# Attention low halves ahead of the feed-forward evacuations, late bounds and moved norms in a fused attention and feed-forward kernel

## The chip, the cores and the metric

One core of a Trainium2 chip runs the whole program. The metric is the time on the device in microseconds (us), as the median of several runs. TensorE (PE) multiplies and transposes, VectorE (DVE), ScalarE (ACT) and GpSimd (POOL) work beside it, and SyncE (SP) issues most DMAs. Each engine takes its instructions strictly in the order in which the program emitted them.

## The reference

The queries are averaged in pairs, so that each of 32 heads (4 batches of 8) has 576 queries against 1152 keys of dimension 64. After the softmax the heads of a batch are laid side by side (512 columns), normalized, and put through a feed-forward layer of width 2048 with a residual.

```python
q_pool = q.reshape(B, H, S // 2, 2, D).mean(axis=3)
scores = scale * np.matmul(q_pool, k.transpose(0, 1, 3, 2))
attn = np.exp(scores - np.max(scores, axis=-1, keepdims=True))
attn = attn / (np.sum(attn, axis=-1, keepdims=True) + 1e-09)
x = np.matmul(attn, v)                      # (4, 8, 576, 64) -> (4, 576, 512)
xn = (x - mu) / np.sqrt(var + 1e-06) * g_ln
out = x + np.maximum(xn @ w_ch1, 0.0) @ w_ch2
```

## The kernel before

**Work.** Every fp32 operand of a matmul is split into a scaled fp16 high half and an fp16 low half, and three products (high by high, high by low, low by high) stand for one. The heads go in 16 pairs p (`HP` = 4 pairs a batch), and a pair has `C` = 9 blocks of 128 queries, so there are 144 attention steps i = 9 p + j. `step(i)` writes out one step for all engines.

**A step.** VectorE takes the row maximum of the scores (`emit_max`, line 399) and makes the exponential's bias `nb` (line 404). ScalarE does the exponential (line 413) and the high half (`emit_hi`, line 427). The low half (`emit_lo`) falls on GpSimd for j = 2, 5, 8 (first a multiplication by 2^15 in place, line 254, then the subtraction, line 434), else on VectorE (line 436). SyncE then issues a transposing DMA, and four steps later TensorE multiplies with the values (`emit_pv`, line 482). In the first 36 steps (`on_pe`, pairs 0 to 3) TensorE transposes the probabilities instead (line 446), ScalarE copies them out (line 452), the product comes out turned and is turned back (`emit_turn`, line 498), and the result is scaled by 1/sum (line 530, then line 537 on ScalarE). VectorE converts the weights in these steps (`w_conv`, through `drip`, line 111).

**Order on TensorE** from step 36 on: scores of block i + 1 (lines 380 and 388), a reduction matmul for a pair's bounds if one is due (lines 206 and 215, `reds`), the product with the values, transposes for a coming pair's keys and queries (`prep_k`, `prep_q`, lines 294, 298, 323, 333), one piece of feed-forward work (`some_units`: `l1` line 618, `l2` line 650), then what `todo` holds: loads, bounds on ScalarE (line 190), and transposes of a normalized block (`ln_t`, line 581).

**Evacuations.** What TensorE leaves in PSUM in step i is collected in `evacs` and written out by `flush` in step i + 1, ahead of the exponential. There are two free banks, 6 and 7 (`bank()`), for transposes, units and norms together; a second-layer unit holds its bank over two steps. Scores use three banks for even and three for odd steps. The product with the values and the two reduction matmuls lie in columns 128 to 386 of the third of these, whose first 128 columns are the end of the scores (line 388).

**Bounds.** `all_max` turns a pair's three partial sums on TensorE (line 206), VectorE takes their maximum (line 209) and spreads it over a small diagonal `dg` (line 210), TensorE multiplies it with ones (line 215), and `scales` makes powers of two of it, which the transposes of keys and queries and the values need.

**Norms.** Once the eight pieces of a block of 128 rows are there, `norm` takes statistics on VectorE (line 563), GpSimd normalizes, and two steps later `ln_t` transposes. Blocks are called t = 0 to 3 for a batch; t = 1 and t = 3 release feed-forward units. After step 143 only feed-forward work is left.

Of the kernel before, what the change touches and what calls it, by code (L numbers as in the profile page):

```python
# [24 lines left out]
def tile_pooled_attention_moe(  # L25
# [18 lines left out]
    nc = tc.nc  # L44
# [150 lines left out]
    def all_max(src, n, then):  # L195

        mx = sm_p.tile([3, 1], FP32, tag="mx3", name="mx3")
        dg = sm_p.tile([3, 3], FP32, tag="dg", name="dg")

        def place():  # L200
            u = this[0] if on_pe(this[0]) else pv_slot[0]
            return psum[:, 3 * (u % 2) + 2, 258:386]

        def one():
            ps = place()
            nc.tensor.transpose(ps[0:n], src, ident)

            def evac():
                nc.vector.tensor_reduce(mx[0:n], ps[0:n], axis=AX.X, op=ALU.max)
                nc.vector.tensor_scalar(dg[0:n, 0:n], ident[0:n, 0:n], mx[0:n], None, op0=ALU.mult)  # L210
            return evac

        def two():
            ps = place()
            nc.tensor.matmul(out=ps[:, 0:n], lhsT=ones3[0:n], rhs=dg[0:n, 0:n], start=True, stop=True)
            return lambda: then(ps[:, 0:n])

        return one, two
# [12 lines left out]
    def scales(p, top, a=0, b=3, both=False):  # L231
# [12 lines left out]
        if a == 0:  # L244
            v.scalar_tensor_tensor(
                sc[:, 0:1], e[:, 0:1], 2.0 ** -32, e[:, 1:2], op0=ALU.mult, op1=ALU.mult
            )
            if on_pe(p * C):
                v.scalar_tensor_tensor(
                    sc[:, 1:2], e[:, 0:1], -(2.0 ** -32), e[:, 1:2], op0=ALU.mult, op1=ALU.mult  # L250
                )

# [87 lines left out]

    def preps_of(p):
        if p < JOINT:
            return PREPS
        if p % 2:
            return [x for x in PREPS if x[0] is prep_k]
        x = PREPS + ((prep_q, 3), (prep_q, 4))
        return x if p != HP else x[:3] + (x[4], x[3]) + x[5:]
# [47 lines left out]
    def emit_max(i):  # L395
# [5 lines left out]
        if on_pe(i):  # L401
            st["mx"] = mx
        else:
            nc.vector.tensor_scalar(nb, mx, sc[:, 0:1], -1.0, op0=ALU.mult, op1=ALU.mult)  # L404

# [18 lines left out]
    def emit_hi(i):  # L424
        st = steps[i]
        hl = st["hl"] = p_p.tile([128, 2, S], FP16, tag="hl", name="hl", bufs=3)
        nc.scalar.activation(out=hl[:, 0], in_=st["pe"], func=ACTF.Copy, scale=2.0 ** 15)  # L427

    def emit_lo(i):
        st = steps[i]  # L430
        hl = st["hl"]
        if low_on_pool(i):
            scaled(st["pe"], st["pe"], 2.0 ** 15)
            nc.gpsimd.tensor_tensor(hl[:, 1], st["pe"], hl[:, 0], op=ALU.subtract)  # L434
# [54 lines left out]

    turned, scaled_out = deque(), deque()  # L490

    def emit_turn(n, ot, i):
# [6 lines left out]
        one, two = evac_pv(n, ps)  # L499
        found.append(one)  # L500
        scaled_out.extend((two, lambda: evacuated(n)))

# [3 lines left out]
    def evac_pv(i, ps):  # L506
# [28 lines left out]
        def two():  # L535
            for u in range(m):
                nc.scalar.activation(  # L537
                    out=x[:, 64 * u:64 * u + 64], in_=ps[o:o + n, 65 * u:65 * u + 64],
                    func=ACTF.Copy, scale=r[:, u:u + 1],
                )  # L540

# [50 lines left out]
    units, preps = deque(), deque()  # L592
    evacs = []

    def flush():
        mine, evacs[:] = list(evacs), []
        waiting.clear()
        for fn in mine:
            fn()
            drip()  # L600
# [227 lines left out]
    for p in range(1, NP):  # L828
# [5 lines left out]
        else:  # L834
            lk = i0 - 2 if p % 2 or not ahead else i0 - 3
        at(lk, load, p, "k", nc.sync)
        at(i0 - ahead, load, p, "v", nc.sync)
        at(i0 + 1 if old else i0, bound, p, "k")
        if p == 1:
# [26 lines left out]
        for n, (fn, u) in enumerate(preps_of(p)):  # L866
            if p == JOINT - 1 and n > 3:
                n -= 1
            pre(i0 + 4 + n + late, lambda fn=fn, p=p, u=u: preps.append((fn, p, u)))
# [46 lines left out]
    def norm(i):  # L916

        if not norms or norms[0][1] % 2 == 0 and norms[0][0] != "h" and not room["xn"]:
            return
        b, t = norms.popleft()  # L920
        st = {}
# [13 lines left out]
        def transpose():  # L935
            evacs.extend(ln_t(st, dst))

# [34 lines left out]
    def some_units(i):  # L972
        for _ in range(1 if i < NSTEP + 5 else 2):
            if units and w_done[units[0][0]] >= units[0][1]:
                evacs.extend(units.popleft()[2]())

    def a_piece(i):
        pieces.extend(ready.pop(i, ()))
        for u in range(2 if len(pieces) > 2 and not on_pe(i) else 1):
            if pieces:  # L980
# [10 lines left out]
                evacs.extend(evac_pv(n, ps))  # L991
                evacs.append(lambda n=n: evacuated(n))

    def step(i):
# [14 lines left out]
        if on_pe(i):  # L1009
# [4 lines left out]
            emit_exp(i)  # L1014
        while scaled_out:
            scaled_out.popleft()()
        if i + 1 < NSTEP:
# [11 lines left out]
        else:  # L1029
            flush()  # L1030
            if live:
                emit_exp(i)
                emit_hi(i)
        if 0 <= i - 1 < NSTEP and not on_pe(i - 1):
            emit_lo(i - 1)
            steps.pop(i - 1)
            drip()
        norm(i)
        while soon or len(fill) > 3:
            drip()  # L1040
        if on_pe(i):
            emit_t(i)
            if reds:
                found.append(reds.popleft()())
        elif reds:
            evacs.append(reds.popleft()())
# [3 lines left out]
        if not on_pe(i):  # L1050
            if not first:
                a_piece(i)
            for _ in range(max(len(preps), 1)):
                a_prep()
            some_units(i)
        for fn, a in todo.pop(i, ()):
            fn(*a)
# [6 lines left out]
    with tc.manual_schedule():  # L1064
# [50 lines left out]
        i = 0  # L1115
        while i < NSTEP + 20 or units or evacs or norms:
            step(i)
# [30 lines left out]
```

## Time and profile before

| | |
|---|---|
| time, median of 3 runs | 913.89 us (908.51 to 914.88) |
| the profiled execution's own time | 909.41 us |
| its span, first to last instruction | 907.4 us |
| mean granted TensorE clock | 0.983 |
| TensorE busy (matmul) | 826.9 us, 91% |
| VectorE, ScalarE, GpSimd busy | 624.7, 569.6, 361.6 us (69%, 63%, 40%) |
| the chain that ended last, by engine | PE 40%, DVE 31%, ACT 16%, DMA 5%, issue 5%, POOL 2% |

An engine's busy time is the sum over its instructions in one profiled execution, and its share is taken of the span. The granted clock is 1.00 at 2.4 GHz and 0.50 at 1.2 GHz. An idle time in brackets behind an instruction is the engine's wait just before it, with the instruction that ended it.

### The profile page before, as it was taken

The page shows a single profiled execution, that of the slowest core. Times are in us where ns is not written, and L with a number is a line of the kernel's source. Part 1 is how long each engine was busy: PE and PEld are TensorE (multiplying, and loading weights), DVE is VectorE, ACT ScalarE, POOL GpSimd, SP SyncE. Part 2 cuts the span into 40 slices and gives each one's busy share as a digit, 9 for nine tenths or more (in the row PEclk, how much of TensorE's full clock was granted, in tenths as well). Part 3 has the DMA queues.
Part 4 walks back from the last instruction along what each step waited for, and adds up shares of the span by engine and source line. Part 5 has one row for each costly group of instructions (what it writes and reads, how often), then busy time and mean ns, then how long its engine had stood idle before and what let it go on. Part 6 is the DMA issues. An engine that isn't in the chain of part 4 may idle for free.

```text
span 907.4 us, 21663 instructions
## 1 busy us (share of the span) xinstructions
PE 826.9 (91%) x9180; PEld 584.8 (64%) x9180; DVE 624.7 (69%) x1087; ACT 569.6 (63%) x850; POOL 361.6 (40%) x324
## 2 busy tenths in 40 slices
PE   8998897998789988797999999898989999999997
PEld 6787776776546564654666666466657576766764
DVE  3688989797877786576777777877777777641211
ACT  4998696887657756566766667576767766511110
POOL 3020927257859726262633334444624342400000
PEclk9999899899999999898999999999999999999999
DMA  7374425304676877776796969587888876600001
GB/s 191 136 213 127 148 84 163 119 26 94 121 163 129 185 140 143 164 155 136 147 176 114 194 134 186 111 179 132 162 157 147 162 129 131 131 20 12 13 12 24
DMA packets 276017, 115.97 MB, mean 128 GB/s; under 512 B 259280, under 2 KB 259280, under 8 KB 275920
## 3 DMA queue, kind: packets, MB, share of 16 engines
q1 hardware_dynamic: 275568, 113.70, 59.2%
q8 instruction: 72, 1.18, 0.6%
q10 hardware_dynamic: 352, 0.88, 0.4%
q14 instruction: 25, 0.20, 0.1%
HBM read 46.14 MB, written 4.72 MB: 56 GB/s over the span
## 4 chain that ended last, share of the span: by engine, by line
PE 40%; DVE 31%; ACT 16%; DMA 5%; issue 5%; POOL 2%; SPq 0%; ACTq 0%; POOLq 0%; DVEq 0%
PE psum L650 12%; PE psum L618 10%; DVE mx L399 9%; DVE hl L436 6%; ACT pe L413 4%; PE psum L470 4%; PE psum L482 4%; DMA pt<-hl 3%; PE psum L380 3%; DVE ht L632 3%; PE psum L446 2%; DVE stage L111 2%; ACT ht L631 2%; ACT qt L283 2%; DVE dg L210 1%
## 5 line engine op out<-in xcount | busy, mean ns | idle before, releaser
L413 ACT ACTIVATE pe<-psum,nb,sc 128x1152 f32<-128x1152 f32 x144 | 188.9, 1312 | 36.8 <-DVE nb L404 26.1
L399 DVE TENSOR_REDUCE mx<-psum 128x1 f32<-128x1152 f32 x144 | 194.3, 1349 | 25.3 <-PE psum L482 12.9
L650 PE MATMUL psum<-wsl,ht 128*128 128x512 f16 x864 | 197.8, 381 | 1.9 <-DVE xb L663 0.8
L618 PEld LDWEIGHTS <-wsl 128*128 128x128 f16 x1920 | 172.6, 99 | 24.1 <-issue 4.4
L618 PE MATMUL psum<-xn,wsl 128*128 128x256 f16 x1536 | 180.3, 276 | 1.5 <-DVE ht L632 0.8
L650 PEld LDWEIGHTS <-ht 128*128 128x128 f16 x864 | 83.0, 98 | 92.3 <-issue 4.7
L427 ACT ACTIVATE hl<-pe 128x1152 f16<-128x1152 f32 x108 | 125.7, 1163 | 9.8 <-DMA pt<-hl 6.5
L380 PE MATMUL psum<-kt,qt 64*128 64x512 f16 (+1 forms) x960 | 121.8, 380 | 3.2 <-ACT pe L413 2.3
L482 PE MATMUL psum<-vt,pt 128*128 128x65 f16 (+1 forms) x3240 | 118.4, 194 | 0.0
L482 PEld LDWEIGHTS <-pt 128*128 128x128 f16 (+1 forms) x3240 | 110.3, 101 | 2.3 <-issue 0.2
L436 DVE SCALAR_TENSOR_TENSOR hl<-pe,hl 128x1152 f16<-128x1152 f32 x72 | 108.8, 1512 | 3.5 <-ACT hl L427 3.5
L537 ACT ACTIVATE xb<-psum,r 128x64 f32<-128x64 f32 x128 | 39.4, 308 | 113.7 <-DVE r L533 110.3
L254 POOL TENSOR_SCALAR pe<-pe 128x1152 f32<-128x1152 f32 x36 | 42.1, 1169 | 163.0 <-ACT hl L427 151.0
L632 DVE SCALAR_TENSOR_TENSOR ht<-psum,ht 128x512 f16<-128x512 f32 x72 | 49.7, 690 | 75.1 <-ACT ht L631 74.7
L631 ACT ACTIVATE ht<-psum 128x512 f16<-128x512 f32 x72 | 42.8, 594 | 88.9 <-PE psum L618 88.7
L434 POOL TENSOR_TENSOR hl<-pe,hl 128x1152 f16<-128x1152 f32 x36 | 86.4, 2399 | 3.0
L470 PE MATMUL psum<-pt,vt 128*65 128x128 f32 (+1 forms) x720 | 80.5, 269 | 1.4 <-DVE qt L280 1.4
L470 PEld LDWEIGHTS psum<-pt,vt 128*65 128x65 f32 x720 | 74.6, 142 | 1.8 <-DVE qt L280 1.8
L380 PEld LDWEIGHTS <-qt 64*128 64x128 f16 (+1 forms) x960 | 34.3, 96 | 55.7 <-issue 36.2
L388 PEld LDWEIGHTS <-qt 128*128 128x128 f16 (+1 forms) x320 | 17.9, 99 | 72.5 <-issue 72.0
L280 DVE SCALAR_TENSOR_TENSOR qt<-psum,s,qt 128x512 f16<-128x512 f32 (+2 forms) x43 | 28.5, 663 | 42.7 <-ACT qt L283 42.7
L388 PE MATMUL psum<-kt,qt 128*128 128x128 f16 (+1 forms) x320 | 41.4, 226 | 12.1 <-ACT xb L537 10.5
(119 smaller groups left out, 1021.9 us busy)
## 6 DMA issues: line engine op xcount, KB each, us to landing
stage<-in_moe_w_ch_dram SPq DMA_DIRECT2D x32, 512.0 KB, 5.1
kr<-in_k_dram SPq DMA_DIRECT2D x16, 576.0 KB, 4.7
qraw<-in_q_dram SPq DMA_DIRECT2D x31, 288.0 KB, 5.0
vr<-in_v_dram SPq DMA_DIRECT2D x15, 576.0 KB, 4.9
out_dram<-xb SPq DMA_DIRECT2D x32, 128.0 KB, 2.4
pt<-hl SPq DMA_TRANSPOSE x108, 4.6
kr<-in_k_dram SPq DMA_DIRECT2D x16, 64.0 KB, 4.3
vr<-in_v_dram ACTq DMA_DIRECT2D x1, 576.0 KB, 6.8
```

The lines of the kernel that those rows point to most:

```text
L380: nc.tensor.matmul(out=sp[o:o + w, c0:c0 + 512], lhsT=qt[r:r + 64, qa, c:c + w], rhs=kt[r:r + 64, ka, h], start=(a == 0), stop=(a == 2),)
L399: nc.vector.tensor_reduce(mx, st["s"], axis=AX.X, op=ALU.max)
L413: nc.scalar.activation(out=st["pe"], in_=st["s"], func=ACTF.Exp, scale=pair[i // C]["sc"][:, 0:1], bias=st["nb"],)
L427: nc.scalar.activation(out=hl[:, 0], in_=st["pe"], func=ACTF.Copy, scale=2.0 ** 15)
L434: nc.gpsimd.tensor_tensor(hl[:, 1], st["pe"], hl[:, 0], op=ALU.subtract)
L436: nc.vector.scalar_tensor_tensor(hl[:, 1], st["pe"], 2.0 ** 15, hl[:, 0], op0=ALU.mult, op1=ALU.subtract)
L470: nc.tensor.matmul(out=ps[0:65, q0:q0 + w], lhsT=vt[:, h, c], rhs=pt[:, 128 * u + q0:128 * u + q0 + w], start=(u == 0), stop=(u == C - 1),)
L482: nc.tensor.matmul(out=dst[:, 0:n], lhsT=lhsT, rhs=rhs, start=(u == 0 and lhsT is hi and n == 65), stop=(u == C - 1 and lhsT is lo), skip_ ...
L618: nc.tensor.matmul(out=ps[:, o:o + n], lhsT=wsl[:, 8 * w + cc, wa, f * 128:f * 128 + 128], rhs=xn[:, xa * KD + cc, 0:n], start=(m == 0), s ...
L631: lambda: nc.scalar.activation(out=hi, in_=pv, func=ACTF.Relu),
L632: lambda: nc.vector.scalar_tensor_tensor(lo, pv, 0.0, hi, op0=ALU.max, op1=ALU.subtract),
L650: nc.tensor.matmul(out=ps, lhsT=hv[0][:, ha, f, t * 128:t * 128 + 128], rhs=wsl[:, 8 * w + 4 + f // 2, wa, (f % 2) * DM:(f % 2) * DM + DM] ...
```

## The change

`flush` now has two lists: `evacs` (product with the values, transposes of keys and queries) goes first, then the attention's low half of step i - 1, then `lates` (units, norms, and bounds from step 54 on). From step 54 on (`JOINT` = 6 pairs) the bounds' reduction matmuls are emitted behind the unit. `dg` is made from PSUM in one operation with two tensor inputs. In the first 36 steps 1/sum is applied on VectorE, right after it is formed. On GpSimd's blocks the factor 2^15 goes into the exponential's bias, so the multiplication on line 254 falls away. Pair 5's transposes come one a step, its second key transposes last; pair 6's loads of keys and values move two steps and one step back, the bound of its keys one; the last two query transposes of a pair of pairs come one step later; norms with t > 1 wait until i % 9 is at least 5.

```diff
             def evac():
                 nc.vector.tensor_reduce(mx[0:n], ps[0:n], axis=AX.X, op=ALU.max)
-                nc.vector.tensor_scalar(dg[0:n, 0:n], ident[0:n, 0:n], mx[0:n], None, op0=ALU.mult)
+                nc.vector.scalar_tensor_tensor(
+                    dg[0:n, 0:n], ps[0:n, 0:n], mx[0:n], ident[0:n, 0:n], op0=ALU.max, op1=ALU.mult
+                )
...
-            if on_pe(p * C):
-                v.scalar_tensor_tensor(
-                    sc[:, 1:2], e[:, 0:1], -(2.0 ** -32), e[:, 1:2], op0=ALU.mult, op1=ALU.mult
-                )
+            v.scalar_tensor_tensor(
+                sc[:, 1:2], e[:, 0:1], -(2.0 ** -32), e[:, 1:2], op0=ALU.mult, op1=ALU.mult
+            )
...
     def preps_of(p):
+        if p == JOINT - 1:
+            return PREPS[:3] + PREPS[4:] + PREPS[3:4]
...
-            nc.vector.tensor_scalar(nb, mx, sc[:, 0:1], -1.0, op0=ALU.mult, op1=ALU.mult)
+            up = 15 * math.log(2) if low_on_pool(i) else 0.0
+            nc.vector.tensor_scalar(nb, mx, sc[:, 1:2], up, op0=ALU.mult, op1=ALU.add)
...
-        nc.scalar.activation(out=hl[:, 0], in_=st["pe"], func=ACTF.Copy, scale=2.0 ** 15)
+        up = 1.0 if low_on_pool(i) else 2.0 ** 15
+        nc.scalar.activation(out=hl[:, 0], in_=st["pe"], func=ACTF.Copy, scale=up)
...
         if low_on_pool(i):
-            scaled(st["pe"], st["pe"], 2.0 ** 15)
             nc.gpsimd.tensor_tensor(hl[:, 1], st["pe"], hl[:, 0], op=ALU.subtract)
...
-        found.append(one)
-        scaled_out.extend((two, lambda: evacuated(n)))
+        found.extend((one, two, lambda: evacuated(n)))
...
-                nc.scalar.activation(
-                    out=x[:, 64 * u:64 * u + 64], in_=ps[o:o + n, 65 * u:65 * u + 64],
-                    func=ACTF.Copy, scale=r[:, u:u + 1],
-                )
+                src, dst = ps[o:o + n, 65 * u:65 * u + 64], x[:, 64 * u:64 * u + 64]
+                if on_pe(i):
+                    nc.vector.tensor_scalar(dst, src, r[:, u:u + 1], None, op0=ALU.mult)
+                else:
+                    nc.scalar.activation(out=dst, in_=src, func=ACTF.Copy, scale=r[:, u:u + 1])
...
-    evacs = []
-
-    def flush():
-        mine, evacs[:] = list(evacs), []
+    evacs, lates = [], []
+
+    def flush(between=None):
+        first, last = list(evacs), list(lates)
+        evacs.clear()
+        lates.clear()
         waiting.clear()
-        for fn in mine:
+        for fn in first:
+            fn()
+            drip()
+        if between:
+            between()
+        for fn in last:
             fn()
             drip()
...
-            lk = i0 - 2 if p % 2 or not ahead else i0 - 3
+            lk = i0 - 3 * ahead + p % 2
         at(lk, load, p, "k", nc.sync)
-        at(i0 - ahead, load, p, "v", nc.sync)
-        at(i0 + 1 if old else i0, bound, p, "k")
+        at(i0 if old else i0 + 1 - 2 * ahead, load, p, "v", nc.sync)
+        at(i0 if ahead else i0 + 1, bound, p, "k")
...
         for n, (fn, u) in enumerate(preps_of(p)):
-            if p == JOINT - 1 and n > 3:
-                n -= 1
+            if u > 2:
+                n += 1
             pre(i0 + 4 + n + late, lambda fn=fn, p=p, u=u: preps.append((fn, p, u)))
...
-        b, t = norms.popleft()
+        b, t = norms[0]
+        if i < NSTEP and (b == "h" or t > 1) and i % C < 5:
+            return
+        norms.popleft()
...
         def transpose():
-            evacs.extend(ln_t(st, dst))
+            lates.extend(ln_t(st, dst))
...
             if units and w_done[units[0][0]] >= units[0][1]:
-                evacs.extend(units.popleft()[2]())
+                lates.extend(units.popleft()[2]())
...
+    def low(n):
+        if 0 <= n < NSTEP and not on_pe(n):
+            emit_lo(n)
+            steps.pop(n)
+            drip()
...
-            flush()
+            flush(lambda: low(i - 1))
             if live:
                 emit_exp(i)
                 emit_hi(i)
-        if 0 <= i - 1 < NSTEP and not on_pe(i - 1):
-            emit_lo(i - 1)
-            steps.pop(i - 1)
-            drip()
...
-        elif reds:
+        elif reds and i < JOINT * C:
             evacs.append(reds.popleft()())
...
             some_units(i)
+            if reds and i >= JOINT * C:
+                lates.append(reds.popleft()())
```

## Rows read from the trace of the kernel before

**Rows 1.** Windows: stretch, length, busy time and instructions by engine, granted clock, DMA.
```profile
63.00:120.00 57.00, 49.60 (x485) 41.66 (x483) 50.10 (x77) 46.35 (x88) 25.36 (x20) 0.94 0.40 125
...
340.00:390.00 50.00, 42.76 (x500) 27.66 (x498) 31.68 (x58) 31.02 (x41) 23.30 (x17) 0.93 0.73 147
...
690.00:740.00 50.00, 49.78 (x614) 34.27 (x610) 38.90 (x70) 36.78 (x51) 17.31 (x14) 1.00 0.84 154
```
**Rows 2.** Waits over the span: total us, times, longest us.
```profile
DVE ht L632 <- ACT ht L631: 74.7, 48, 3.4
...
PE psum L215 <- DVE dg L210: 11.5, 7, 2.6
...
PE psum L388 <- ACT xb L537: 10.5, 11, 1.9
...
PE psum L298 <- DVE kt L280: 9.4, 7, 2.8
...
PE psum L581 <- DVE qt L280: 3.9, 4, 1.9
...
PE psum L581 <- DVE xb L663: 2.7, 1, 2.7
```
**Rows 3.** Timeline 468 to 492, steps 83 to 87: start, length, instruction, [idle before].
```profile
468.74 2.78 PE L618 MATMUL psum<-xn,wsl 128*128 128x256 f16 x24
...
471.35 2.38 DVE L210 TENSOR_SCALAR dg<-ident,mx 3x3 f32<-3x3 f32 x1
471.36 2.36 POOL L434 TENSOR_TENSOR hl<-pe,hl 128x1152 f16<-128x1152 f32 x1
...
473.79 0.38 PE L215 MATMUL psum<-dg,ones 3*128 3x3 f32 x2 [1.27 <-DVE dg L210]
...
485.64 0.44 PE L298 MATMUL psum<-ident,kr 128*128 128x128 f32 x2 [1.26 <-DVE kt L280]
```
**Rows 4.** Four lines' instructions: shortest, median, longest ns, first and last start.
```profile
L399 DVE TENSOR_REDUCE mx<-psum x144: 1323/1348/1359, 16.0 to 778.2; 128x1 f32<-128x1152 f32 x144
...
L210 DVE TENSOR_SCALAR dg<-ident,mx x20: 201/217/2385, 11.0 to 713.5; 3x3 f32<-3x3 f32 x13, 1x1 f32<-1x1 f32 x4, 2x2 f32<-2x2 f32 x3
...
L632 DVE SCALAR_TENSOR_TENSOR ht<-psum,ht x72: 679/692/694, 222.0 to 893.0; 128x512 f16<-128x512 f32 x72
...
L436 DVE SCALAR_TENSOR_TENSOR hl<-pe,hl x72: 1345/1349/3066, 210.0 to 781.7; 128x1152 f16<-128x1152 f32 x72
```
**Rows 5.** Timeline 331 to 432, TensorE, steps 65, 73 and 75.
```profile
366.80 0.38 PE L206 MATMUL psum<-ident,acc 128*3 128x128 f32 x1 [3.90 <-ACT kt L190]
...
368.46 4.52 PE L618 MATMUL psum<-xn,wsl 128*128 128x256 f16 x24
...
417.43 0.63 PE L581 MATMUL psum<-ident,xs 128*128 128x128 f32 x4 [2.69 <-DVE xb L663]
...
423.50 0.58 PE L215 MATMUL psum<-dg,ones 3*128 3x3 f32 x2 [2.23 <-DVE dg L210]
...
425.47 5.01 PE L618 MATMUL psum<-xn,wsl 128*128 128x256 f16 x24
```
**Rows 6.** Timeline 226 to 262, TensorE, step 43.
```profile
252.58 0.90 PE L323 MATMUL psum<-ident,qraw 64*128 64x64 f32 x6 [4.18 <-DVE kt L280]
```
**Rows 7.** Timeline 66 to 86, step 11.
```profile
67.37 1.31 ACT L413 ACTIVATE pe<-psum,nb,sc 128x1152 f32<-128x1152 f32 x1
...
68.94 0.27 PE L388 MATMUL psum<-kt,qt 128*128 128x128 f16 x2 [0.79 <-ACT xb L537]
...
69.05 1.15 PE L446 MATMUL psum<-ident,pe 128*128 128x128 f32 x9
```
**Rows 8.** Costliest groups of the page: busy us, mean ns, idle before.
```profile
L537 ACT ACTIVATE xb<-psum,r 128x64 f32<-128x64 f32 x128 | 39.4, 308 | 113.7 <-DVE r L533 110.3
L254 POOL TENSOR_SCALAR pe<-pe 128x1152 f32<-128x1152 f32 x36 | 42.1, 1169 | 163.0 <-ACT hl L427 151.0
```
**Rows 9.** DMA issues of the page: count, size, us to landing.
```profile
vr<-in_v_dram SPq DMA_DIRECT2D x15, 576.0 KB, 4.9
```

More of the change, by code (lines that the diff above doesn't have):

```diff
@@ L1 @@
+import math
 from collections import deque
@@ L488, in emit_pv @@
         return ps
-    turned, scaled_out = deque(), deque()
+    turned = deque()
     def emit_turn(n, ot, i):
@@ L1014, in step @@
             emit_exp(i)
-        while scaled_out:
-            scaled_out.popleft()()
         if i + 1 < NSTEP:
@@ L1115, in tile_pooled_attention_moe @@
         i = 0
-        while i < NSTEP + 20 or units or evacs or norms:
+        while i < NSTEP + 20 or units or evacs or lates or norms:
             step(i)
```

## The prediction

> **What bounds the kernel now.** I read the windows first [rows 1]. Between 690 and 740 us, late in the attention, TensorE is busy for 49.78 of 50.00 us, with VectorE at 38.90 and ScalarE at 36.78: a step can be written so that TensorE never waits, and neither of the others stands in the way. Between 340 and 390 us the same kind of steps leaves TensorE idle for 7.24 us, at a granted clock of 0.93. So TensorE's work sets the time, and the change, which takes nothing from that work, can win only its gaps and the stretches at 1.2 GHz. The gaps are in the list of waits [rows 2]. Each has a name: TensorE waits at line 215 for `dg` (11.5 us, 7 times), at line 388 for ScalarE's scaling of a block in the same bank (10.5 us, 11 times), at line 298 for the low half of the first keys (9.4 us, 7 times), at line 581 for a bank that the last transposes or unit still hold (6.6 us in two rows). Last I read the timelines of single steps [rows 3, 5 to 7] to see what would be late next.
>
> In the stage with both attention and feed-forward work, VectorE is the one that is late, though it is busy only 78% even in the best window. It stands still for ScalarE's ReLU before each unit's low half (74.7 us, 48 times [rows 2]), with the attention's low half queued behind that wait, and behind this the next step's maximum. Now the edits, with their share against the profiled execution's 909.41 us.
>
> **Bounds: `dg` and the matmuls behind the unit.** `dg` has 3 columns and a median of 217 ns, but a longest of 2385 [rows 4]. In step 84 it took 2.38 us exactly beside GpSimd's 2.36 us of line 434, and TensorE, whose line 215 stood ahead of the values and the unit, waited 1.27 us [rows 3]; in step 75 it waited 2.23 [rows 5]. The new form reads PSUM and one tensor in SBUF. The nearest row of that form is line 632, and all its 72 instructions lie between 679 and 694 ns, many of them beside GpSimd [rows 4]; so I take 0.2 us for the new one (0.2 to 2.4 as bounds). The matmuls still run, but behind 2.78 us of unit, by when `dg` is ready. The 7 waits of line 215 go: 11.5. In step 65 line 206 waited 3.90 us for a bound on ScalarE [rows 5]; behind the unit it would not hold up TensorE, but ScalarE's exponential stays late, so I count half, 2. **Together -13** (0 to -15.4).
>
> **TensorE's clock.** The unit behind these two waits ran at 1.2 GHz: 24 matmuls in 4.52 and 5.01 us against 2.78 in step 83 [rows 3, 5], so 1.7 and 2.2 us lost on the unit alone, and about a third more on the step's other 2 us of matmuls. In both cases TensorE had stood still for over 2 us just before. If the waits go, these two stretches should too: **-4** (0 to -5.5).
>
> **Pair 5's transposes one a step.** Today its second keys and a third of its queries come in the same step, while a second-layer unit holds the other bank, and the queries waited 4.18 us for the keys' low half [rows 6]. That goes. The price is pair 6's loads: keys now come at the end of step 45 and their bound at the end of 46, values at the end of 46 and their bound at the end of 47, one step from issue to use instead of two. SyncE also waits there for the last key transposes, with a transposing DMA queued behind it that nobody needs for four steps. A value load lands 4.9 us after its issue [rows 9], about as long as a step; ScalarE, with the exponential queued behind the bound, may wait 0 to 4.9 us twice. I take 1.5. **-2.7** (-4.2 to +5.6).
>
> **Norms and late query transposes.** In step 73 the block's transposes waited 2.69 us because the query transposes and the unit had both banks [rows 5]; in all line 581 waits 6.6 us in these rows [rows 2]. Moving the query transposes out of j = 1, and the norms of t = 2 and 3 so that `ln_t` falls on j = 7 and 8, where the coming odd pair has no transposes left, clears all but the wait of t = 0 (two steps behind j = 6, beside a coming even pair's query transposes). The norm's statistics and GpSimd's part move along. The units of t = 3 come two steps later, but the 16 of t = 1 last longer than that. **-5** (0 to -6.6).
>
> **Low half first.** The low half needs ScalarE's `hi` of the step before, always there ahead of this step's ReLU, which is queued behind it on ScalarE; so it fills the wait of line 632. I worked steps 84 to 87 through by hand with the durations of the rows. VectorE reaches the first keys' low half 1.3 us sooner relative to TensorE, since the `dg` stretch is gone, the bounds' scales no longer stand ahead of 1/sum, and the wait is filled; line 298's 1.26 us [rows 3] falls away. In return the unit's low half ends up to 1.35 us (line 436 [rows 4]) later, and the next unit, in the same bank, waits 0.2. As line 298's waits are partly the echo of line 215's, of their 9.4 us I count **-5** (0 to -9.4), and **+2** for units that wait for their bank (0 to +10).
>
> **First 36 steps: 1/sum on VectorE.** The 10.5 us of line 388 look like a gain, but only part is one. In step 11 the scores' end waited 0.79 us, yet the transposes behind it need the exponential, which ended at 68.68, 0.37 us before they began [rows 7]: the exponential is late next. So 0.3 to 0.5 us come back each time, and ScalarE, which paces that chain, loses 308 ns a step [rows 8]. VectorE gains 40 small operations, between `dg`'s 0.2 and the 512 columns' 0.69 us [rows 4]; I take 0.25 for 64 columns, 10 us in all, and it is busy 50.10 of 57 us there [rows 1]. Where weights are converted beside GpSimd's splits, this is paid in full. **-2.5** (-10 to +10).
>
> **2^15 in the bias.** 36 operations of 1.17 us leave GpSimd [rows 8], whose blocks reach the transposing DMA that much sooner, four steps ahead of use: **-1** (0 to -3). The bias costs what it cost. The 12 more operations on `sc` take about 0.2 us each, in VectorE's idle time.
>
> Sum: -13 - 4 - 2.7 - 5 - 5 + 2 - 2.5 - 1 = -31.2, so 878.2 for a profiled execution. The median of the runs is 4.5 above that execution's own time: **883**.
>
> **Rivals.** *The bank is held.* In the rows line 388 waits for readers of other columns of its bank [rows 2]. From step 54 on the bounds' results are read from such a bank in `lates`, behind the low half and the unit, where they used to be read first. If the scores two steps on have to wait, as line 388 waits today (10.5 / 11 = 0.95 us), 9 pairs times 2 reads cost 17 us: a gain of 14, 900. Against it: by hand the scales' first read in step 85 comes about 4 us before those scores. The Trainium skill, "PSUM — Partial Sum Buffer", section "Terms", says that two engines may not be on one bank at once, whatever the columns, so a wait has to separate them; that is the rule which speaks against late bounds, and the trace's waits of line 388 agree with it.
>
> *The gaps only move.* If the gaps show just where VectorE's lateness is noticed, only work that leaves VectorE counts: some six stretches of `dg` by 2.2 us are gone, and 10 us come in the first 36 steps, mostly hidden. A gain of about 9: 905. For it: much of line 298 is an echo. Against: 78% busy in the window without gaps [rows 1].
>
> *The unit's bank becomes the wait (slower).* A step lasts 5.33 us in the mean (144 maxima start between 16.0 and 778.2 [rows 4]), of which a unit is 2.78; in a step with transposes the next unit thus needs the last one's bank about 2.55 us after that one ended. With the low half first, VectorE goes through the maximum 1.35 us, three small operations 0.6, a wait for ScalarE's scaling and high half of about 1.0, the transposes' low half 0.7, the attention's 1.35 and the unit's 0.69 [rows 4, 8]: 5.7 in all. So TensorE waits whenever the maximum starts less than 3.15 us before the unit ends. If VectorE's lead stays short of that by a whole low half, 1.35 us are paid in each of 90 steps x 11/18 with transposes x 2/3 with VectorE's low half x 3/4 with something to evacuate = 27: 37 us, and the clock's 4 are not won either. 37 - 27 = +10: 924. Against: in the steps worked by hand the lead is about 3 us and the wait 0.2, and behind second-layer units there is none.
>
> **How the numbers follow.** Forecast, a gain of 17 to 45 us: 0.62. Bank held, 900: 0.10. Gaps move, 905: 0.12. Unit's bank, 924 and above: 0.09. More than 45 us, if nearly every wait goes, and the stretches at 1.2 GHz in the first 36 steps too (0.94 between 63 and 120 us [rows 1]): 0.07. A measurement of this kernel can tell about 1%, 9 us, from no change. Faster by more: the forecast, the bank's case, the best case and 0.01 of the gaps' case, 0.80; within 1%: the rest of the gaps' case, 0.11; slower: 0.09. The range, 866 to 906, takes in the first rivals and leaves out the fourth case and what is better than a gain of 48. It is about what the terms' bounds give when they don't all fall on one side.
>
> **What would show it.** Right: `dg` never above 0.3 us and no wait at line 215 from step 54 on; line 323's 4 us and line 581's 2.7 gone; line 632 waits for ScalarE far less than 74.7 us; the windows from 340 to 440 at a clock of 1.00; TensorE's busy share at 93% or more. The bank's case would show as waits of line 388 for lines 210 or 235; the unit's as waits of lines 618 and 650 for 632 and 663; the first stage's as VectorE over 95% busy between 63 and 177 us, with no fewer microseconds there. I would be wrong above all if the short stalls of today hide a VectorE that is late by as much for another reason.

## The result, and the profile after

Ten runs of the changed kernel had a median of 921.54 us (919.22 to 925.95), ten of the kernel before on the same chip 912.86. The ratio is 1.011 (95% interval 1.008 to 1.014): slower by about 1%, where 883 us and a gain had been forecast. The profiled execution took 925.95 us, the longest of the ten. Two runs beside the experiments below, one of 2440.31 us (late bounds in another bank) and one of 1339.76 us (the kernel before), stand in no time and no ratio.

From the page of the changed kernel, its span and each engine's busy time:

```profile
span 924.1 us, 21573 instructions
...
PE 840.3 (91%) x9180; PEld 592.3 (64%) x9180; DVE 621.3 (67%) x1139; ACT 563.1 (61%) x810; POOL 315.3 (34%) x288
```

GpSimd is busy 46 us less than before, 42 of them the multiplication by 2^15 that is gone [rows 8]. VectorE is busy 3 us less, and TensorE 13 us more for the same matmuls, at a granted clock of 0.970 against 0.983. As a pair the two pages exaggerate: their executions differ by 16.5 us, the medians by 8.7. Over the ten runs the clock was 0.970 to 0.979, over the nine runs of the kernel before beside the first experiments 0.973 to 0.979. So the pages alone don't say where the time went. Windows of the changed kernel (stretch, length, busy time and instructions by engine, clock, DMA):

```profile
340.00:390.00 50.00, 46.50 (x562) 30.74 (x563) 37.45 (x74) 36.23 (x49) 20.14 (x15) 0.97 0.95 167
...
490.00:540.00 50.00, 44.37 (x498) 29.37 (x497) 32.89 (x63) 30.39 (x41) 16.99 (x19) 0.95 0.81 147
...
690.00:740.00 50.00, 47.36 (x574) 30.86 (x572) 34.90 (x66) 34.54 (x48) 13.98 (x12) 1.00 0.77 142
```

Between 340 and 390 us TensorE is busier than it was [rows 1]. Between 690 and 740, where it had been busy for 49.78 of 50 us [rows 1], 2.64 us are now idle, and VectorE is busy 4 us less as well: both stand still more. The waits over the span (engine, line, tile, what it waited for: total us, times, longest) name the place:

```profile
POOL vt L256 <- DVE s L246: 62.1, 7, 12.8
DVE ht L644 <- ACT ht L643: 58.2, 35, 4.2
...
DVE mx L403 <- PE psum L218: 26.5, 10, 4.4
DVE mx L403 <- PE psum L207: 21.2, 10, 3.7
DVE mx L403 <- PE psum L487: 20.9, 30, 2.7
ACT pe L418 <- DVE dg L211: 16.0, 9, 4.0
ACT pe L418 <- DVE red L238: 15.8, 8, 4.2
...
PE psum L630 <- DVE ht L644: 13.0, 12, 1.9
```

Lines 207 and 218 are the bounds' two matmuls (206 and 215 before), 403 is the next step's row maximum, 418 its exponential. Twenty times VectorE's maximum stands still for a bounds matmul, 47.7 us in all. Eighteen of these waits, 43.5 us, come from step 54 on; the other two come before it, where the bounds still go ahead. The wait of the unit's low half for its ReLU (line 644) fell from 74.7 [rows 2] to 58.2 us.

The timeline of the changed kernel (start, length, instruction, idle time before it) shows how one pair's bounds do this, in steps 92 and 93:

```profile
520.28 2.78 PE L630 MATMUL psum<-xn,wsl 128*128 128x256 f16 x24
...
522.90 0.27 PE L207 MATMUL psum<-ident,acc 128*3 128x128 f32 x1
523.21 1.36 DVE L403 TENSOR_REDUCE mx<-psum 128x1 f32<-128x1152 f32 x1 [3.67 <-PE psum L207]
...
526.97 0.44 PE L335 MATMUL psum<-ident,qraw 128*128 128x128 f32 x2 [1.87 <-DVE qt L282]
...
527.57 4.45 PE L630 MATMUL psum<-xn,wsl 128*128 128x256 f16 x24 [0.16 <-DVE ht L644]
527.73 0.21 DVE L211 SCALAR_TENSOR_TENSOR dg<-psum,mx,ident 3x3 f32<-3x3 f32 x1
527.98 1.31 ACT L418 ACTIVATE pe<-psum,nb,sc 128x1152 f32<-128x1152 f32 x1 [1.36 <-DVE dg L211]
...
531.94 0.38 PE L218 MATMUL psum<-dg,ones 3*128 3x3 f32 x2
532.36 1.36 DVE L403 TENSOR_REDUCE mx<-psum 128x1 f32<-128x1152 f32 x1 [4.42 <-PE psum L218]
...
537.50 4.45 PE L630 MATMUL psum<-xn,wsl 128*128 128x256 f16 x24 [1.21 <-DVE ht L644]
```

The bounds' product lies in columns 258 to 386 of the third bank of the slot that holds the scores of step i + 1. The maximum of step i + 1 reads the first 128 columns of that bank. Emitted behind the unit, the matmul is also ahead of that maximum, so the maximum waits until the unit is through: 3.67 and 4.42 us, and it starts within 0.05 us of the matmul's end. The exponential, which reads the same bank, then waits for VectorE to take the bounds' result out of it. VectorE, late by a unit, makes TensorE wait in turn (1.87 and 1.21 us in the rows). The unit behind each of these waits takes 4.45 us for its 24 matmuls instead of 2.78; between 527.50 and 532.00 us the granted clock was 0.62, so part of the unit ran at 1.2 GHz.

### The profile page after: what moved, and what is told of

Same layout as the page of the kernel before. It is cut to its first block, busy times and chain, and to the rows that moved or that the text cites. A ratio compares the mean times of both kernels' runs of the same rounds, so it can differ in the third digit from the quotient of the medians.

```text
span 924.1 us, 21573 instructions
## 1 busy us (share of the span) xinstructions
PE 840.3 (91%) x9180; PEld 592.3 (64%) x9180; DVE 621.3 (67%) x1139; ACT 563.1 (61%) x810; POOL 315.3 (34%) x288
## 4 chain that ended last, share of the span: by engine, by line
PE 53%; DVE 30%; ACT 11%; issue 3%; DMA 2%; POOL 1%; SPq 0%; ACTq 0%; DVEq 0%; POOLq 0%
PE psum L630 19%; PE psum L662 13%; DVE mx L403 8%; PE psum L487 6%; DVE hl L441 5%; PE psum L384 5%; DVE stage L112 4%; PE psum L475 3%; ACT pe L418 3%; PE psum L451 2%; DVE qt L282 2%; DVE wsl L112 2%; PE psum L392 2%; DVE kt L282 1%; ACT qt L285 1%
## 5 line engine op out<-in xcount | busy, mean ns | idle before, releaser
L630 PEld LDWEIGHTS <-wsl 128*128 128x128 f16 x1920 | 178.5, 102 | 49.8 <-issue 25.9
L630 PE MATMUL psum<-xn,wsl 128*128 128x256 f16 x1536 | 188.8, 284 | 21.1 <-DVE ht L644 11.8
L441 DVE SCALAR_TENSOR_TENSOR hl<-pe,hl 128x1152 f16<-128x1152 f32 x72 | 106.5, 1479 | 0.0
L644 DVE SCALAR_TENSOR_TENSOR ht<-psum,ht 128x512 f16<-128x512 f32 x72 | 49.5, 688 | 58.5 <-ACT ht L643 58.2
L545 ACT ACTIVATE xb<-psum,r 128x64 f32<-128x64 f32 x96 | 29.7, 309 | 97.0 <-DVE r L537 93.5
L451 PE MATMUL psum<-ident,pe 128*128 128x128 f32 x324 | 45.6, 289 | 9.6 <-ACT pe L418 9.5
L457 ACT COPY pt<-psum 128x512 f32<-128x512 f32 x72 | 44.4, 638 | 11.3 <-PE psum L451 5.4
```

Of the source, the lines that this page charges most:

```text
L441: nc.vector.scalar_tensor_tensor(hl[:, 1], st["pe"], 2.0 ** 15, hl[:, 0], op0=ALU.mult, op1=ALU.subtract)
L451: nc.tensor.transpose(st["s"][:, n], st["pe"][:, n], ident)
L630: nc.tensor.matmul(out=ps[:, o:o + n], lhsT=wsl[:, 8 * w + cc, wa, f * 128:f * 128 + 128], rhs=xn[:, xa * KD + cc, 0:n], start=(m == 0), s ...
```

## The experiments

All kernels compute the full result. Ratios are to the kernel before, run beside each on the same chip; where two kernels are compared, the difference of their ratios is taken of 912 us.

**Bounds ahead again.** The changed kernel without its late bounds.

```diff
-        elif reds and i < JOINT * C:
+        elif reds:
             evacs.append(reds.popleft()())
...
-            if reds and i >= JOINT * C:
-                lates.append(reds.popleft()())
```

> The changed kernel with the bounds' two reduction matmuls back ahead of the values, and their evacuation back in the first list; all else as changed. Theory A: behind the unit they lie in the bank that the next step's maximum reads, so VectorE waits at 20 places for a whole unit (47.7 us in the changed kernel's waits), and TensorE pays some 30 us of it within the two steps that follow: 890 us (885 to 900), no wait of the maximum for lines 207 or 218 over 0.5 us. Theory B: the low half first makes VectorE late and the bounds only show it: 912 to 922 us, and the gaps of TensorE behind the bounds stay.

887.88 us, ratio 0.975 (0.972 to 0.978). The one step turns a loss of 1.1% into a gain of 2.5%; it costs 33 us. Without that step the change gains 23 us, where 31 had been forecast with it. The stretch from the maximum of step 54 to the last one holds the same 5312 matmuls in both kernels. First it in the changed kernel, then in this one (columns as in the windows above):

```profile
311.30:794.60 483.30, 439.57 (x5312) 291.89 (x5313) 340.91 (x633) 321.09 (x424) 165.08 (x148) 0.98 0.81 149
```
```profile
307.70:756.40 448.70, 426.44 (x5312) 284.29 (x5313) 341.25 (x633) 321.06 (x424) 170.53 (x148) 1.00 0.88 160
```

Of the 34.6 us between them, 21.5 are TensorE standing still for longer and 13.1 are the same matmuls taking longer, at a clock of 0.98 against 1.00. Windows and waits of the kernel with bounds ahead:

```profile
340.00:390.00 50.00, 48.30 (x607) 31.12 (x605) 37.60 (x70) 38.24 (x50) 25.19 (x20) 1.00 0.94 163
...
490.00:540.00 50.00, 46.81 (x573) 30.45 (x572) 35.27 (x65) 36.00 (x48) 18.47 (x13) 1.00 0.95 179
```
```profile
DVE mx L403 <- PE psum L487: 29.3, 41, 2.7
...
PE psum L630 <- DVE ht L644: 8.7, 11, 1.9
...
PE psum L207 <- ACT kt L191: 1.6, 3, 1.0
PE psum L218 <- DVE dg L211: 1.6, 2, 0.9
```

The maximum still waits for the values (line 487), which lie in that bank too, but these come ahead of the unit. The last two rows say what the late place could have won at most: in this kernel, bounds ahead make TensorE wait for 3.2 us in all.

**Late bounds alone, in the kernel before.**

```diff
-        elif reds:
+        elif reds and i < JOINT * C:
...
             some_units(i)
+            if reds and i >= JOINT * C:
+                evacs.append(reds.popleft()())
```

> The kernel before with one edit: from step 54 on the bounds' matmuls are emitted behind the unit. Theory A: the same waits of the maximum come up without any other edit, 20 of about 2.4 us; TensorE's waits at line 215 for dg go (some 11 us), about 34 us of new gaps come: 925 to 940 us. Theory B: a gain, 900 to 910 us.

916.03 us, 1.006 (1.003 to 1.009): a small loss. The maximum waits 13.2 us for line 215 and 10.1 for line 206, where it waited 0.9 and 1.4 before. These are half the waits of the changed kernel, and the loss is below the 925 to 940 us that were expected.

**Late bounds in another bank.** The product goes to the bank of the step's own scores, which its maximum and exponential have already read.

```diff
-            u = this[0] if on_pe(this[0]) else pv_slot[0]
+            u = this[0] if on_pe(this[0]) else pv_slot[0] - (this[0] >= JOINT * C)
```

> The changed kernel, with the late bounds' matmuls put in the bank of the step's own scores, which its exponential has read by then, instead of the next step's. Theory A: the maximum no longer waits, 885 to 900 us, unless the end of the scores two steps on (line 392) now waits for the evacuation of the bounds in the late list, 18 times 0.95 us: then 900 to 912. Theory B: as changed, 915 to 925.

901.06 us, 0.990 (0.986 to 0.993): some 19 of the 33 us come back, with the matmuls still behind the unit. So the place in TensorE's queue costs through the bank that the matmuls write. The 14 us that are left go with the same wait, which has another victim:

```profile
PE psum L487 <- DVE dg L211: 9.8, 9, 2.9
PE psum L487 <- DVE red L238: 5.6, 9, 1.1
```

The values of the next step go into that bank, and TensorE now waits 15.4 us until the bounds' results have been read out. Late bounds also make the scales late, and GpSimd waits longer for them (line 256: 62.1 us in the changed kernel, 17.0 with bounds ahead). Here it still waits 35.0 us; how much of the 14 us that costs is not shown.

**Which half of the step costs: the matmuls' place or the late reading.** First the matmuls late, read first as they used to be; then the matmuls ahead, read last.

```diff
             if reds and i >= JOINT * C:
-                lates.append(reds.popleft()())
+                evacs.append(reds.popleft()())
```

> The changed kernel with the bounds' matmuls behind the unit, as in it, but their results read first by VectorE in the next step again. If the matmuls' place behind the unit costs nearly all (the next maximum, which reads their bank, stands behind them), 912 to 921. If the late reading costs most (the exponential, which reads that bank too, waits for it), 890 to 900.

```diff
-        elif reds and i < JOINT * C:
-            evacs.append(reds.popleft()())
+        elif reds:
+            (evacs if i < JOINT * C else lates).append(reds.popleft()())
...
-            if reds and i >= JOINT * C:
-                lates.append(reds.popleft()())
```

> The counterpart: the bounds' matmuls ahead of the values and the unit again, their results read last by VectorE as in the changed kernel. If the matmuls' place costs nearly all, 886 to 895, and the waits of the maximum for the bounds' matmuls are gone. If the late reading costs most, 905 to 915, and the exponential waits for the bounds' results as long as in the changed kernel (16.0 and 15.8 us).

Read first: 930.87 us, 1.022 (1.019 to 1.025), slower than the changed kernel, and above what either theory gave. Read last: 890.58 us, 0.977 (0.973 to 0.981), not to be told from the bounds ahead. So the matmuls' place, in that bank, is the whole cost, and the late reading is none of it. With late matmuls it is even better to read late, by 10 us. Read first, the results and the scales stand ahead of the low halves on VectorE, and TensorE's units wait 21.0 us for the unit's low half (line 644), where they wait 14.0 in the changed kernel; that this is the 10 us fits, but no run tests it by itself. Of the two kernels, the waits with the matmuls ahead and read last:

```profile
DVE mx L403 <- PE psum L487: 30.6, 40, 2.7
...
POOL vt L256 <- DVE s L246: 28.8, 7, 5.0
...
ACT pe L418 <- DVE red L238: 3.7, 6, 1.2
```

Of the maximum's waits for lines 207 and 218 only the two before step 54 are left, 1.7 us each. The exponential's two rows, 16.0 and 15.8 us, became 2.3 and 3.7. The late read leaves traces, GpSimd's wait for the scales (28.8, with bounds read first 17.0) and TensorE's for `dg` (3.7 against 1.6), but no price that the time shows.

**How the price depends on the rest.** The forecast had priced the step as a gain; here it cost 33 us, alone 6. In the kernel before, with the new `dg`, and with `dg` and the low half first, each with bounds ahead and late:

```diff
+                nc.vector.scalar_tensor_tensor(
+                    dg[0:n, 0:n], ps[0:n, 0:n], mx[0:n], ident[0:n, 0:n], op0=ALU.max, op1=ALU.mult
+                )
...
+            flush(lambda: low(i - 1))
```

> The kernel before with the new form of dg alone. If dg's stretch beside GpSimd is on the path, as TensorE's waits at line 215 say (11.5 us, and part of line 298's behind them): 8 to 14 us less than before, 897 to 903, dg at 0.21 us throughout. If the gaps only move to where VectorE is late next: within 4 us of before.

898.77 us, 0.988 (0.986 to 0.991).

> The kernel before with the new dg and the bounds behind the unit, nothing else. If the late bounds' price is the bank alone, independent of the rest: as e2, 913 to 919, since behind the unit dg's stretch no longer held TensorE there, which is some 17 us over e5. If e2 was held up by its slow dg: 900 to 908.

913.35 us, 1.003 (1.000 to 1.006).

> The kernel before with the new dg and the low half first, bounds ahead. If the two add up (12.0 and 4.8 us alone): 891 to 896. If the low half first needs the other edits: 897 to 901. Against e1 (887.9) it gives what sums, norms, pair 5's order and the bias are worth together.

904.54 us, 0.994 (0.991 to 0.996).

> The kernel before with the new dg, the low half first, and the bounds behind the unit in the late list. If the low half first makes the bank's price larger, since VectorE is then earlier at the maximum and the held work lies behind it (33.7 us between the changed kernel and e1): 918 to 928. If the price is the same 17 us with either order: 908 to 914.

920.35 us, 1.014 (1.009 to 1.020).

Then in the changed kernel with the norms' edit taken back, with bounds ahead and late, and the same for pair 5's:

```diff
-        b, t = norms[0]
-        if i < NSTEP and (b == "h" or t > 1) and i % C < 5:
-            return
-        norms.popleft()
+        b, t = norms.popleft()
...
-            if u > 2:
-                n += 1
```

> The kernel of e1 with the norms and the last two query transposes back where they stood before. If their move is worth what was forecast (5 us): 891 to 895, and waits of line 586 of about 6 us come back. If the other edits had already cleared those waits: 886 to 890.

898.01 us, 0.989 (0.985 to 0.994).

> The changed kernel with its late bounds kept and the edit on norms and late query transposes taken back. The same kernel with the bounds ahead again was measured at 898.0 us. If the moved norms are what makes late bounds dear (33.7 us in the full change, about 15 without them), this run comes 13 to 18 us behind that: 911 to 916. If the price is high whatever the norms do, it comes 28 us or more behind: 926 to 935.

922.83 us, 1.011 (1.004 to 1.018).

```diff
-        if p == JOINT - 1:
-            return PREPS[:3] + PREPS[4:] + PREPS[3:4]
...
-            lk = i0 - 3 * ahead + p % 2
+            lk = i0 - 2 if p % 2 or not ahead else i0 - 3
...
-        at(i0 if old else i0 + 1 - 2 * ahead, load, p, "v", nc.sync)
-        at(i0 if ahead else i0 + 1, bound, p, "k")
+        at(i0 - ahead, load, p, "v", nc.sync)
+        at(i0 + 1 if old else i0, bound, p, "k")
...
+            if p == JOINT - 1 and n > 3:
+                n -= 1
```

> The changed kernel with the bounds ahead again (887.9) and pair 5's transposes, with pair 6's loads, as they were. If the edit moves time between pairs only, as the starts of the maxima show (4.6 us won in pair 4, 5 lost in pair 5), 886 to 890. If it gains the 2.7 us of the forecast, 890 to 892.

890.67 us, 0.978 (0.974 to 0.983).

> The changed kernel with late bounds kept and pair 5's transposes, with pair 6's loads, as they were. If pair 6's later keys and bound are what makes late bounds dear, this gains 10 us or more: below 912. If the edit only shifts time between pairs 4, 5 and 6, 919 to 924.

921.45 us, 1.012 (1.007 to 1.017).

Seven pairs with and without late bounds, in the order of the maximum's wait for the bounds' two lines (read from the trace of the late kernel of each pair):

| late bounds in | maximum waits, us | step costs, us |
|---|---|---|
| the kernel before | 23.3 | 6 |
| with `dg` | 27.6 | 13 |
| the change without the norms' edit | 39.3 | 20 |
| with `dg` and low half first | 41.3 | 19 |
| the change without pair 5's edit | 47.6 | 31 |
| the change | 47.7 | 33 |
| the change, bounds read first | 50.1 | 43 |

The last pair is read first, late and ahead. In each wait, 2.2 to 4.4 us come from the two steps before 54. The cost is the difference of two ratios, with about 0.5% (5 us) of doubt on each. No single edit makes the step dear. An edit that helps VectorE lets it reach the maximum sooner, and so stand longer before a matmul whose time TensorE sets: that is how I read the list. The waits grow by 27 us down it, the cost by 37. That the rest is hidden in gaps that the slower kernels have anyway, and uncovered as these close, fits the list but was not measured by itself.

**Pair 6's key load and bound.** The maxima's starts show that the changed kernel wins 4.5 us in pair 4 and loses 5.1 in pair 5 (steps 36 to 53). In its trace ScalarE waits 4.03 us for these keys, and a unit 3.95 us:

```profile
268.84 2.62 POOL L172 TENSOR_TENSOR qraw<-qraw 128x1152 f32<-128x1152 f32 x1
268.90 3.78 DVE L441 SCALAR_TENSOR_TENSOR hl<-pe,hl 128x1152 f16<-128x1152 f32 x1
...
269.55 0.58 SPq L124 DMA_DIRECT2D kr<-in_k_dram  x1
...
274.64 1.16 ACT L191 ACTIVATE kt<-kr 128x1152 f16<-128x1152 f32 x1 [4.03 <-DMA kr<-in_k_dram]
...
275.91 0.74 DVE L675 SCALAR_TENSOR_TENSOR xb<-psum,inv,xb 128x512 f32<-128x512 f32 x1
...
276.70 5.28 PE L630 MATMUL psum<-xn,wsl 128*128 128x256 f16 x24 [3.95 <-DVE xb L675]
```

Two ways out: the bound a step later in the changed kernel, or the load on ScalarE's queue in the one with bounds ahead.

```diff
-        at(i0 if ahead else i0 + 1, bound, p, "k")
+        at(i0 if ahead else i0 + (1 if old else 2), bound, p, "k")
```

> The changed kernel with pair 6's bound of the keys one step later (47 instead of 46). In the changed kernel ScalarE waits 4.03 us there for the load, TensorE 3.95 us, and 6.8 us at 1.2 GHz follow. If the load is the cause: 4 to 7 us less than the changed kernel, 915 to 918; if three bounds in one step hold ScalarE as long: the same as changed.

920.74 us, 1.011 (1.008 to 1.014).

```diff
-        at(lk, load, p, "k", nc.sync)
+        at(lk, load, p, "k", nc.scalar if p == JOINT else nc.sync)
```

> The kernel of e1 with pair 6's key load issued from ScalarE's queue, where it doesn't stand behind the transposing DMA of step 44's low half. If the late load is what takes back the gain of pair 5's new order (ScalarE's 4.0 us, TensorE's 4.0 us and a stretch at 1.2 GHz behind it): 3 to 6 us less than e1, 882 to 885. If the three bounds in a row are the cause: as e1, 886 to 890.

887.30 us, 0.976 (0.974 to 0.978). Neither brings a gain. The first takes ScalarE's wait for the load away, and the unit still waits 3.96 us: that wait was not the load's. It ends with VectorE's line 675, and VectorE is late for it by its own low half, which takes 3.78 us beside GpSimd's line 172, and 3.77 with the later bound, where others take 1.35. In the second the longest low half there takes 1.94 us and the unit waits 1.86. There step 54 begins 288.4 us after step 0 instead of 292.0; 1.7 of these 3.6 us are left at the last maximum, and the span is 1.0 us shorter.

**The low half's place.** Alone in the kernel before, and taken back in the kernel with bounds ahead.

```diff
...
-            flush()
+            flush(lambda: low(i - 1))
             if live:
                 emit_exp(i)
                 emit_hi(i)
-        if 0 <= i - 1 < NSTEP and not on_pe(i - 1):
-            emit_lo(i - 1)
...
```

> The kernel before with the order of the evacuations alone: transposes and values first, then the low half, then units and norms. If it fills VectorE's wait for ScalarE's ReLU: 3 to 8 us less, 903 to 908, line 632's waits well under 74.7 us. If the unit's bank becomes the wait: slower than before, waits of lines 618 and 650 for 632 and 663 above 10 us.

905.96 us, 0.996 (0.993 to 0.998).

> The changed kernel with the bounds ahead again (887.9) and the attention's low half behind the evacuations again. If the order of the low half costs 5.8 us in company of the other edits as it did beside dg alone, 879 to 884. If it brings its own 4.8, as it did alone, 891 to 895.

889.88 us, 0.977 (0.972 to 0.983), 2 us behind bounds ahead and within its interval. Alone the edit brings 4 us; on top of the new `dg` it loses 5 (0.994 against 0.988, intervals just apart); in the full set it does nothing that can be measured. First the waits of the kernel with the low half first alone, then one of the kernel with the new `dg` alone (its line 300 is 298):

```profile
DVE ht L639 <- ACT ht L638: 57.9, 39, 2.6
...
PE psum L625 <- DVE ht L639: 6.7, 6, 2.3
...
PE psum L298 <- DVE kt L280: 1.5, 1, 1.5
...
PE psum L215 <- DVE dg L210: 1.3, 2, 0.7
```
```profile
PE psum L300 <- DVE kt L282: 8.7, 7, 2.8
```

Even with the old `dg`, the waits of lines 215 and 298 [rows 2] are down from 20.9 to 2.8 us. In return TensorE's units wait for what VectorE now writes out behind the low half: 18.1 us in all (lines 625 and 657 for 639, 670 and 588), where it was 3.0 before. The new `dg` alone leaves 2.2 us of line 215's waits, but line 298's stay, 8.7 us. So beside the new `dg` the low half first has only some 8 us of waits left to remove, and again adds 15 to the units' (17.9 against 2.8). As an estimate from these rows that makes a gain of 3 alone and a loss of 7 beside `dg`; measured are 4 and 5. Of the loss, 4.8 us lie in pairs 4 and 5: 105.0 us with `dg` and low half first, 100.2 with `dg` alone.

**1/sum on ScalarE again,** with bounds ahead.

```diff
...
-                if on_pe(i):
-                    nc.vector.tensor_scalar(dst, src, r[:, u:u + 1], None, op0=ALU.mult)
-                else:
-                    nc.scalar.activation(out=dst, in_=src, func=ACTF.Copy, scale=r[:, u:u + 1])
+                nc.scalar.activation(out=dst, in_=src, func=ACTF.Copy, scale=r[:, u:u + 1])
...
```

> The kernel of e1 (bounds ahead) with 1/sum of the first 36 steps back on ScalarE. The maxima of the changed kernels reach step 36 some 2 to 4 us later than before. If VectorE's 40 operations cost that: 884 to 887, step 36 reached 2 to 3 us sooner. If they gain, as forecast: 889 to 892.

889.06 us, 0.978 (0.976 to 0.981): 3 us slower, within the intervals. The first 36 steps take the same time (190.2 against 190.6 us from the first maximum to the 37th).

## Why the prediction was wrong

The step that failed is the second half of "Bounds": "The matmuls still run, but behind 2.78 us of unit, by when `dg` is ready." Both halves of that sentence hold, and the conclusion doesn't: it looked at who the matmuls wait for, and not at who waits for the matmuls. Their bank is that of the next scores, the next maximum stood behind them unnoticed, and the place behind the unit costs 33 us where it was booked at none. The rest of the change, with the bounds ahead, gains 23 us.

The rivals. *The bank is held* had the bank, but the wrong end of it: it put the price on the late reading, with line 388 of the scores two steps on as the one who waits, 17 us. The late reading by itself costs nothing measurable, and in the changed kernel line 392 (388 before) waits only for 1/sum of the first 36 steps, 2.8 us. The rule of the Trainium skill, "PSUM — Partial Sum Buffer", section "Terms", that two engines may not be on one bank at once whatever the columns, agrees with the maximum's eighteen waits: of that bank it reads columns 0 to 127, and it stands still for a write to columns 258 to 386. Applied to the write too, and not to the read alone, it would have pointed at the maximum. *The unit's bank becomes the wait* gave 924, near the measured time, but not by what happened. Its waits did come: lines 630 and 662 wait 24.3 us for 644 and 675, against its 37 and 2.5 before. But 19.6 of these remain with bounds ahead, in a kernel that is 2.5% faster. *The gaps only move*, 905, is answered by the same kernel's 888.

The other terms, each with what it measured:

- `dg`, -11.5 of the -13: right. All 20 take 206 to 210 ns (201 to 2385 before [rows 4]), as the first row says, and alone it brings 11 us. In the changed kernel only one of the 20 falls beside work of GpSimd, so the second row, from the kernel with `dg` alone, is the better witness.

```profile
L211 DVE SCALAR_TENSOR_TENSOR dg<-psum,mx,ident x20: 206/207/210, 12.3 to 728.2; 3x3 f32<-3x3 f32 x13, 1x1 f32<-1x1 f32 x4, 2x2 f32<-2x2 f32 x3
```
```profile
L210 DVE SCALAR_TENSOR_TENSOR dg<-psum,mx,ident x20: 206/207/208, 11.4 to 703.5; 3x3 f32<-3x3 f32 x13, 1x1 f32<-1x1 f32 x4, 2x2 f32<-2x2 f32 x3
```

  With the other edits this had already removed the waits for which the matmuls were moved: the move had 3.2 us left to win (7.4 with `dg` alone).
- Clock, -4: seen in the windows. With bounds ahead, all windows from 290 to 880 us show 1.00, and the mean of four runs is 0.986 against 0.977 of the kernel before beside them. It has no price of its own in the runs. In the changed kernel clock was lost instead: 0.95 between 490 and 540 us, and 13.1 us from step 54 on against bounds ahead.
- Norms and late query transposes, -5: mis-sized. Taken back in the kernel with bounds ahead they cost 13 us (0.989 against 0.975), twice the 6.6 us of line 581's waits that the term was counted from.
- Pair 5 one a step, -2.7: 3 us, within the intervals, so neither shown nor refuted. The 4.2 us wait of line 323 went (line 325 now waits 1.8 at most), and pair 5 gave as much back. The load's wait is the smaller part of that: without it, in the kernel with the later bound, pair 5 is 0.8 us shorter. The bound of 0 to 4.9 us for ScalarE's wait held (4.03).
- Low half first, -5 +2: about -4 alone and nothing measurable in the full set. Line 298's waits went, as forecast, but they were no echo of line 215's: 8.7 us stay with `dg` alone. The units' waits for their bank were mis-sized: 15 us more of them alone, outside the bounds of 0 to 10.
- 1/sum on VectorE, -2.5, between bounds of -10 and +10: no measurable effect (3 us, within the intervals).
- 2^15 in the bias, -1: no run tests it by itself.

The terms other than late bounds, as measured one at a time (11, 13, 3, 2, 3), sum to 32 us where the kernel with bounds ahead gains 23. With some 5 us of doubt on each that is no proof of overlap, but `dg` and the low half do fall short: 11 and 4 alone, 6 together. That the gain of 23 comes near the forecast's 31 is partly luck, since the norms gave more and the low half less than their terms. That kernel, 0.975, is the best that was run; none of the further edits tells itself apart from it with a gain.

## What to carry to other kernels

When an instruction is moved back on its engine, list who waits for it, not only for what it waits: everything emitted later that touches its buffer's bank, in whatever columns, is moved back with it. Ask also whether another part of the same change has already removed the wait that the move is for. Price each edit in the company of the others: here one step cost 6 us alone and 33 in the set.

## What the runs showed of the hardware

The three-column operation that stretched to 2.385 us beside GpSimd, with both tensors in SBUF, took 0.206 to 0.210 us in all 20 cases, once its first operand was in PSUM and it had two tensor inputs. In the kernel with `dg` alone, six of the 20 fall into GpSimd's 2.37 us subtraction, as here, and none takes longer than 0.208 us:

```profile
515.08 2.37 POOL L436 TENSOR_TENSOR hl<-pe,hl 128x1152 f16<-128x1152 f32 x1
...
515.25 0.21 DVE L210 SCALAR_TENSOR_TENSOR dg<-psum,mx,ident 3x3 f32<-3x3 f32 x1
```

Which of the two differences does it was not separated. The Trainium skill, "SBUF — State Buffer", section "SBUF: two separate sides", says that VectorE and GpSimd share a pair of ports, which whoever comes first holds for a whole instruction, and that of VectorE's operations only those in a two-port mode or with two inputs in SBUF take part; these durations and the old 2.38 us beside GpSimd's 2.36 [rows 3] agree with it.

The waits that made TensorE stand still cost more than their own length: from step 54 on the late bounds cost 21.5 us of standing still and 13.1 us of slower matmuls, and in the timeline above the units behind TensorE's waits took 4.45 us instead of 2.78.
